# When the first expert's weights are loaded in an mLSTM-plus-MoE kernel: w1 in quarters in steps 19 and 21, w2 in step 22

## The chip, the cores and the metric

The kernel runs on one core of a Trainium2 chip. Times are device microseconds (us) of that core. The runs shown give the median of three executions; one more look comes from the hardware profiler, whose page and trace cover one execution.

## What is computed

The program has two halves. The first is an mLSTM cell over 4 batches, 8 heads, 768 time steps and heads of 40 elements. The second treats its output as 3072 token rows of 320 elements and sends each row to one of 8 experts by a hash of its token id; an expert is two matrix products with a ReLU between them. Cut to its core:

```python
for t in range(S):                       # S = 768, state C is 40 x 40 per head
    m_new = maximum(f_gate[t] + m, i_gate[t])
    f_stab, i_stab = exp(f_gate[t] + m - m_new), exp(i_gate[t] - m_new)
    C = f_stab * C + i_stab * outer(v[t], k[t])
    n = f_stab * n + i_stab * k[t]
    y[t] = sigmoid(o_gate[t]) * (C @ q[t]) / maximum(abs(n @ q[t]), 1)
x = y.reshape(3072, 320)                 # (batch, time) x (head, dim)
e = token_ids * 2654435761 % 8
out[rows of e] = relu(x[rows of e] @ w1[e]) @ w2[e]   # w1: 320x1024, w2: 1024x320
```

## The kernel before

**The cell** is cut into 24 steps (`NT`), one for each batch and each block of 128 time positions; step `s` works on batch `s % 4` and block `s // 4`. All engines run one hand-written order, a Python loop over `s`, with no scheduler between. In step `s` TensorE does, in this order: `turn(s + 2)`, which transposes the keys and queries of the block after next (L390); `scores(s + 1)`, the products of keys and queries (L447); `decays(s + 1)`, two products that build the logarithms of the decay weights (L405, tile `ab`) and, from the second block on, one for the queries' decay (L418, tile `xb`); `state(s)`, the update of C (L478); `attend(s)`, the output rows (L499 and L505). `decays` reads a tile called R, which holds rows of gate sums fetched from DRAM by `load_a` (L248). There are three R buffers, and `load_a(s + 3)` is issued in step `s`, so R(22) is fetched in step 19 and R(23) in step 20. VectorE makes `qs` (L422) from `xb`, and `weigh` (L453) multiplies scores by decay weights, which frees the two score tiles `sp0` and `sp1` for the next `scores`. ScalarE takes the exponentials (L414), copies the transposed blocks out (L395) and, in `gate(i)`, turns an output gate into a sigmoid (L438, L439). GpSimd multiplies the gate in (`gated`, L522). The finished rows go to a DRAM table `x_d` (`store`, L525), from SyncE's queue up to block 16 and from GpSimd's after that.

**The loads.** Nearly all DMAs are issued by SyncE (SP), in program order. Step `s` issues, in this order: `load_a(s + 3)`, k and q of block `s + 5`, v of block `s + 4`, the output gate (`og`) of a later block, one store, and then the `pieces` of the step. A load of k, q, v or og is 160 KB in 1024 runs of 160 bytes. The supply of blocks ends near the tail: step 18 has the last k and q, step 19 the last v, step 20 the last R. The program gives SP's DMAs eight completion semaphores in rotation, and each DMA waits for the one eight before it.

**The first expert's weights.** Expert 0 needs w1 (rows 0 to 255 as tile `w1t`, 1024 KB; rows 256 to 319 as `w1c`, two loads of 128 KB) and w2 (`w2t`, 1280 KB). `slices_of(0)` cuts these loads into seven `parts`, and the step loop hangs one into `pieces` of each of steps 17 to 23: w1's upper 128 rows in 17, its lower 128 rows in 18, `w1c` in 19, and a quarter of w2 in each of steps 20 to 23.

**The tail.** In step 20 GpSimd gathers two blocks of expert 0's rows from `x_d` (`xg0`, L110). They are copied by VectorE in step 22 (L886) and transposed by `early_turn` in steps 22 and 23 (L747, copied out at L748). When step 23 is over, `layer1(W[0], ...)` runs for the first 256 rows (L157 and L150): it takes the 1024 columns of w1 in four pairs of 128 (`fp`), from low to high. The expert loop follows: `layer2` for expert 0 (L1042), then for each further expert both layers with seven products in place of eight (L991, L999, L1075), fed by gathers on GpSimd, a pass through DRAM (`x_slots`, `xb`), and the weight loads of `load_weights` on SP.

Of the kernel before, what the change touches and what calls it, by code (L numbers as in the profile page):

```python
# [17 lines left out]
P = 128  # L18
# [4 lines left out]
def kernel(  # L23
# [24 lines left out]
    nc = tc.nc  # L48
# [5 lines left out]
    E, _, F = moe_w1.shape  # L54
# [65 lines left out]
    def slices_of(e):  # L120

        w1t = wpools[0].tile([P, 2, F], F32, name="w1t")
        w1c = wpools[0].tile([P, FB // 2, P], F32, name="w1c")
        w2t = w2pools[0].tile([P, FB, Dm], F32, name="w2t")
        W[e] = w1t, w1c, w2t
        last = moe_w1[e][2 * P :, :].rearrange("d (a two f) -> two d a f", two=2, f=P)
        rows = moe_w2[e].rearrange("(a p) d -> p a d", p=P)

        def part(i):
            if i < 2:  # L130
                nc.sync.dma_start(w1t[:, i], moe_w1[e][i * P : (i + 1) * P, :])
            elif i == 2:
                for j in range(2):
                    nc.sync.dma_start(w1c[j * P // 2 : (j + 1) * P // 2], last[j])
            else:
                r = slice(2 * (i - 3), 2 * (i - 2))
                nc.sync.dma_start(w2t[:, r], rows[:, r])

        return [lambda i=i: part(i) for i in range(7)]

    def layer1(w, xT, h, c0, c1, bank):

# [47 lines left out]
    with tc.tile_pool(name="gates", bufs=1) as gp, \  # L190
# [363 lines left out]
        def route_iotas(i):  # L554
            for ti, tf, pattern, base, mult in list(iotas.values())[i::2]:
                nc.gpsimd.iota(ti[:], pattern=pattern, base=base, channel_multiplier=mult)
                nc.gpsimd.tensor_copy(tf[:], ti[:])
# [140 lines left out]
        def route_table(i):  # L698
            tk = ps.tile([P, 2, NC], F32, name="tk", tag="sp0")
            for t in range(TH):  # L700
                nc.tensor.matmul(tk[:], lhsT=oh_r[:, t, :], rhs=oh_c[:, t], start=(t == 0), stop=(t == TH - 1))
            for part in range(2):
                if i == 0 and part == 0:
                    nc.vector.tensor_copy(tv[:], tk[:, 0])
                else:
                    nc.vector.tensor_tensor(tv[:], tv[:], tk[:, part], op=ALU.add)

        def route_index():
# [17 lines left out]
        pieces = {  # L726
            2: [lambda: route_iotas(0)], 3: [lambda: route_iotas(1), route_consts, route_parts], 4: [route_experts],
            5: [route_chosen], 7: [route_extra, route_masked], 8: [route_rank], 9: [route_high], 10: [route_slots, g2.ends, lambda: g2.split("e")], 11: [route_places],
            20: [route_index], 21: [route_tiles],
        }  # L730
        products = {4: [route_turned], 5: [route_counts]}
        for i in range(8):
            pieces.setdefault(12 + i, []).append(lambda i=i: route_hot(i))
            if i % 2:
                products[12 + i] = [lambda i=i // 2: route_table(i)]
        for i, part in enumerate(slices_of(0)):
            pieces.setdefault(17 + i, []).append(part)
        gates_of = {}
        for i, j in enumerate((4, 5, 6, 6, 7, 8, 8, 9)):
            gates_of.setdefault(j, []).append(i)  # L740
# [368 lines left out]
    with tc.manual_schedule():  # L1109
# [56 lines left out]
        for e in range(E):  # L1166
            g, i = e // EG, e % EG
# [84 lines left out]
```

## Time and profile before

| | |
|---|---|
| median of three runs | 357.02 us (353.64 to 359.27) |
| the profiled execution's own time | 357.02 us |
| its span | 355.2 us |
| TensorE busy | 336.3 us, 95% of the span |
| VectorE / ScalarE / GpSimd busy | 229.8 / 139.4 / 215.1 us |
| DMA traffic | 59.18 MB, mean 167 GB/s |
| mean granted TensorE clock | 0.988 |

Times in the trace count from the start of the span; the run's own time is 1.8 us longer. A busy share is an average over stages with different limits, so the stage around the change, from about 95 to 160 us, has to be read by itself.

### The profile page before, as it was taken

How to read it: one execution, taken by the hardware profiler on the slowest of the kernel's cores; microseconds unless marked ns; L12 is line 12 of the kernel's file. 1: busy time of each engine (PE TensorE's matmuls, PEld its weight loads, DVE VectorE, ACT ScalarE, POOL GpSimd, SP SyncE). 2: the span in 40 equal slices, each digit the busy share in tenths (PEclk: the TensorE clock that was granted, in tenths of full speed). 3: DMA queues.
4: the chain of work that ended last, by engine and by line, in shares of the span. 5: the costliest groups of instructions: out<-in, count | busy, mean ns of one | idle time of the engine just before them, and what ended most of it. 6: DMA issues, size and time to landing. Idle time of an engine off the chain costs nothing.

```text
span 355.2 us, 9214 instructions
## 1 busy us (share of the span) xinstructions
PE 336.3 (95%) x3573; PEld 293.8 (83%) x3573; DVE 229.8 (65%) x512; ACT 139.4 (39%) x325; POOL 215.1 (61%) x301
## 2 busy tenths in 40 slices
PE   7889999999999599999999999999999999999990
PEld 6677898888888476789899899789899899899870
DVE  8867897998888462037675796835776756844510
ACT  6676688776675451021411412301411412312300
POOL 8832778899885346515925938825926918427521
PEclk9999999999999899999999999999999999999997
DMA  6698999989988983679987959587477484000010
GB/s 129 118 195 156 162 200 172 194 175 193 177 165 199 243 239 92 198 201 297 218 247 192 327 103 316 159 215 219 117 208 237 106 235 146 0 34 22 16 40 3
DMA packets 162358, 59.18 MB, mean 167 GB/s; under 512 B 140171, under 2 KB 158119, under 8 KB 162313
## 3 DMA queue, kind: packets, MB, share of 16 engines
q1 hardware_dynamic: 158377, 49.05, 59.8%
q0 software_dynamic: 2832, 9.34, 8.0%
q8 instruction: 29, 0.48, 0.5%
q10 hardware_dynamic: 1104, 0.18, 0.3%
q14 instruction: 16, 0.13, 0.1%
HBM read 46.48 MB, written 12.38 MB: 166 GB/s over the span
## 4 chain that ended last, share of the span: by engine, by line
PE 84%; DMA 4%; issue 4%; DVE 3%; ACT 2%; SPq 1%; POOL 1%; POOLq 0%
PE mh L991 20%; PE mh L1075 13%; PE mh L1042 12%; PE sp L447 6%; PE mh L999 6%; PE tr L390 6%; PE xh L505 5%; PE mh L157 3%; PE ab L405 3%; PE xh L499 3%; PE xh L478 2%; DMA k<-in_k_dram 2%; DMA R<-gate_rows 1%; PE mh L1155 1%; PE xb L418 1%
## 5 line engine op out<-in xcount | busy, mean ns | idle before, releaser
L917 POOL DMA_INDIRECT out_dram<-zo,s_idx x26 | 26.8, 1030 | 69.5 <-issue 47.2
L1042 PE MATMUL mh<-w2t,h 128*128 128x320 f32 x160 | 45.0, 433 | 0.5 <-ACT h L166 0.5
L1042 PEld LDWEIGHTS mh<-w2t,h 128*128 128x128 f32 x160 | 30.0, 190 | 11.8 <-ACT h L166 0.9
L977 DVE TENSOR_TENSOR h<-u,mh 128x416 f32<-128x416 f32 (+1 forms) x56 | 25.4, 475 | 16.6 <-PE mh L999 7.8
L505 PE MATMUL xh<-v,w 128*64 128x41 f32 x768 | 35.6, 225 | 0.0
L414 ACT ACTIVATE w<-ab 128x512 f32<-128x512 f32 x48 | 26.2, 596 | 18.8 <-PE ab L405 17.9
L453 DVE TENSOR_TENSOR w<-sp,w 128x512 f32<-128x512 f32 x48 | 30.8, 681 | 3.6 <-ACT w L414 3.6
L991 PE MATMUL mh<-tx,sw 128*128 128x208 f32 x168 | 31.8, 339 | 0.0
L505 PEld LDWEIGHTS xh<-v,w 128*64 128x64 f32 x768 | 31.8, 141 | 0.0
L991 PEld LDWEIGHTS mh<-tx,sw 128*128 128x128 f32 x168 | 29.7, 190 | 0.0
L447 PE MATMUL sp<-qT,kT 64*128 64x128 f32 x384 | 28.0, 285 | 0.9 <-ACT qT L395 0.9
L110 POOL DMA_INDIRECT xg<-x_rows,g_idx x24 | 23.4, 974 | 9.0 <-issue 6.7
L977 DVE TENSOR_TENSOR u<-m,mh 128x416 f32<-128x416 f32 x28 | 16.5, 588 | 18.7 <-PE mh L991 18.0
L499 PE MATMUL xh<-C,qs 128*64 128x82 f32 x320 | 28.3, 254 | 0.0
L522 POOL TENSOR_TENSOR x<-x,og 128x320 f32<-128x320 f32 x24 | 20.6, 865 | 12.1 <-ACT og L439 10.1
L1075 PE MATMUL mh<-tw,sh 128*128 128x160 f32 x168 | 27.4, 299 | 0.0
L447 PEld LDWEIGHTS sp<-qT,kT 64*128 64x128 f32 x384 | 23.4, 187 | 4.8 <-issue 2.3
L1075 PEld LDWEIGHTS mh<-tw,sh 128*128 128x128 f32 x168 | 24.3, 190 | 0.0
L991 PE MATMUL mh<-xT,w1t 128*128 128x208 f32 x112 | 23.1, 339 | 0.0
L488 POOL TENSOR_TENSOR C<-C,add 64x164 f32<-64x164 f32 x32 | 16.3, 509 | 9.9 <-ACT add L482 8.6
L913 ACT COPY zo<-mh 128x320 f32<-128x320 f32 x12 | 5.1, 426 | 42.6 <-PE mh L1042 27.3
L422 DVE TENSOR_TENSOR qs<-qT,xb 128x512 f32<-128x512 f32 x20 | 13.7, 683 | 12.6 <-PE xb L418 12.6
(241 smaller groups left out, 775.3 us busy)
## 6 DMA issues: line engine op xcount, KB each, us to landing
w2t<-in_moe_w_dram SPq DMA_DIRECT2D x7, 1280.0 KB
w1t<-in_moe_w_dram SPq DMA_DIRECT2D x7, 1024.0 KB
xb<-x_slots SPq DMA_DIRECT2D x84, 52.0 KB
k<-in_k_dram SPq DMA_DIRECT2D x24, 160.0 KB
v<-in_v_dram SPq DMA_DIRECT2D x24, 160.0 KB
og<-in_o_gate_dram SPq DMA_DIRECT2D x24, 160.0 KB
q<-in_q_dram SPq DMA_DIRECT2D x23, 160.0 KB
x_slots<-xg SPq DMA_DIRECT2D x7, 480.0 KB
```

Of the source, the lines that this page charges most:

```text
L110: nc.gpsimd.indirect_dma_start(out=xg, out_offset=None, in_=x_d[:rows, :], in_offset=bass.IndirectOffsetOnAxis(ap=idx, axis=0),)
L390: nc.tensor.transpose(tp[:, j, :], d[what][:, 2 * j : 2 * j + 2, :].rearrange("p h d -> p (h d)"), ident[:])
L414: nc.scalar.activation(w[:, hf], ab[:], AF.Exp)
L447: nc.tensor.matmul(sp[hf][:, j, :], lhsT=d["kT"][r, j, :], rhs=d["qT"][r, j, :], start=True, stop=True)
L453: nc.vector.tensor_tensor(d["w"][:, hf], d["sp"][hf][:], d["w"][:, hf], op=ALU.mult)
L499: nc.tensor.matmul(xh[t, 2 * j : 2 * j + 2, :], lhsT=d["qs"][:, j, t], rhs=Cs[b][c % 2][:, j].rearrange("p h d -> p (h d)"), start=True, s ...
L505: nc.tensor.matmul(hs[t, 2 * j + hf, :], lhsT=d["w"][:, hf, j, t], rhs=d["v"][:, 2 * j + hf, :], start=(c == 0), stop=True, skip_group_che ...
L917: ins = nc.gpsimd.indirect_dma_start(out=out[:, :], out_offset=bass.IndirectOffsetOnAxis(ap=idx, axis=0), in_=zo[:], in_offset=None, bound ...
L977: nc.vector.tensor_tensor(o, a, b, op=ALU.add)
L991: nc.tensor.matmul(pair(bank[n])[:, a], lhsT=lhsT(g + a), rhs=rhs, start=first and a == 0, stop=True, skip_group_check=True,)
L1042: nc.tensor.matmul(zp, lhsT=h[:, fb, j * P : (j + 1) * P], rhs=w[2][:, fb, :], start=(fb == 0), stop=(fb == FB - 1),)
L1075: nc.tensor.matmul(bank[n], lhsT=lhsT(f), rhs=rhs(f), start=first and f == 0, stop=f == FB // 2 - 1, skip_group_check=True,)
```

## The change

The loads of w1's rows 0 to 255 are cut in four: each 128 rows by half of the columns (512 of 1024). The quarters with the low columns are issued in step 19, `w1c` in step 20, the quarters with the high columns in step 21, and all four parts of w2 in step 22. In every step they still stand behind the step's own loads. Nothing is issued in steps 17, 18 and 23 any more.

```diff
         def part(i):
-            if i < 2:
-                nc.sync.dma_start(w1t[:, i], moe_w1[e][i * P : (i + 1) * P, :])
-            elif i == 2:
+            if i < 4:
+                f = slice(i // 2 * F // 2, (i // 2 + 1) * F // 2)
+                nc.sync.dma_start(w1t[:, i % 2, f], moe_w1[e][i % 2 * P : (i % 2 + 1) * P, f])
+            elif i == 4:
                 for j in range(2):
                     nc.sync.dma_start(w1c[j * P // 2 : (j + 1) * P // 2], last[j])
             else:
-                r = slice(2 * (i - 3), 2 * (i - 2))
+                r = slice(2 * (i - 5), 2 * (i - 4))
                 nc.sync.dma_start(w2t[:, r], rows[:, r])
 
-        return [lambda i=i: part(i) for i in range(7)]
+        return [lambda i=i: part(i) for i in (0, 1, 4, 2, 3, 5, 6, 7, 8)]
...
-        for i, part in enumerate(slices_of(0)):
-            pieces.setdefault(17 + i, []).append(part)
+        for s, part in zip((19, 19, 20, 21, 21, 22, 22, 22, 22), slices_of(0)):
+            pieces.setdefault(s, []).append(part)
```

The instructions of the four computing engines and their order are the same in both programs; only SP's order differs:

| step | SP before | SP after |
|---|---|---|
| 17 | R(20), k, q, v, og, store, **w1 upper rows** | R(20), k, q, v, og, store |
| 18 | R(21), k(23), q(23), v(22), og(19), store(16), **w1 lower rows** | R(21), k(23), q(23), v(22), og(19), store(16) |
| 19 | R(22), v(23), og(20), **w1c x2** | R(22), v(23), og(20), **w1 low columns x2** |
| 20 | R(23), og(21), **w2** | R(23), og(21), **w1c x2** |
| 21 | og(22), og(23), **w2** | og(22), og(23), **w1 high columns x2** |
| 22 | **w2** | **w2 x4** |
| 23 | **w2** | nothing |

## The prediction

> **What bounds the kernel now.** I read the page's busy shares first, then TensorE's waits in the stretch of the change, then SP's issues there, then the granted clock.
>
> ```profile
> PE 336.3 (95%) x3573; PEld 293.8 (83%) x3573; DVE 229.8 (65%) x512; ACT 139.4 (39%) x325; POOL 215.1 (61%) x301
> ```
>
> TensorE is busy 95% of the span, so time can come only from its holes. The list of waits of PE between 100 and 140 us has one large one:
>
> ```profile
> PE ab L405 <- DMA R<-gate_rows: 3.6, 1, 3.6
> ```
>
> In the timeline of PE and of SP (start, length, what, idle before) that hole and its history read:
>
> ```profile
> 114.50 0.41 PE L505 MATMUL xh<-v,w 128*64 128x41 f32 x8
> 115.11 0.63 PE L390 MATMUL tr<-ident,k 128*128 128x128 f32 x4 [0.20 <-DMA k<-in_k_dram]
> 116.37 1.16 PE L447 MATMUL sp<-qT,kT 64*128 64x128 f32 x16
> 121.18 0.83 PE L405 MATMUL ab<-R,L 128*64 128x512 bf16 x4 [3.65 <-DMA R<-gate_rows]
> ...
> 126.13 0.62 PE L405 MATMUL ab<-R,L 128*64 128x512 bf16 x4
> ...
> 132.06 1.99 PE L157 MATMUL mh<-xT,w1t 128*128 128x256 f32 x8 [0.28 <-ACT xT L748]
> ```
>
> ```profile
> 107.26 0.42 SPq L131 DMA_DIRECT2D w1t<-in_moe_w_dram  x1
> 107.78 0.33 SPq L248 DMA_DIRECT2D R<-gate_rows  x1
> 108.15 0.59 SPq L237 DMA_DIRECT2D k<-in_k_dram  x1
> 108.79 0.88 SPq L237 DMA_DIRECT2D q<-in_q_dram  x1
> 109.72 4.55 SPq L237 DMA_DIRECT2D v<-in_v_dram  x1
> 114.36 0.53 SPq L233 DMA_DIRECT2D og<-in_o_gate_dram  x1
> 114.99 0.93 SPq L525 DMA_DIRECT2D x_rows<-x  x1
> 115.97 0.42 SPq L131 DMA_DIRECT2D w1t<-in_moe_w_dram  x1
> 116.48 0.31 SPq L248 DMA_DIRECT2D R<-gate_rows  x1
> ```
>
> The reader is to see that R(22), wanted at 117.5, is issued only at 116.48, behind both w1 loads, and that the issue of v(22) holds SP for 4.55 us just after the first w1 load. Last, the table of 2 us stretches (PE, PEld, DVE, ACT, POOL, clock, DMA share, GB/s):
>
> ```profile
> 118.00:120.00 2.00, 0.00 (x0) 0.00 (x0) 0.00 (x0) 1.54 (x4) 1.00 (x2) 1.00 0.89 236
> 122.00:124.00 2.00, 2.00 (x35) 1.86 (x32) 1.52 (x3) 1.48 (x5) 0.97 (x1) 0.50 0.96 227
> ```
>
> After the hole TensorE runs at half clock; the trace's clock record gives 0.5 from 121.46 to 124.87. After 162 us PE has no visible hole until the end, so what is gained by then arrives at the end if the expert's supply moves with it.
>
> [...]R(22) landed at 121.14, just after the w1 load issued before it (120.83). [...]the first w1 load landed on 15 engines by 112.15 and on the last at 114.47, and k(23) behind it by 112.97 and at 114.97. [...]3.65 us idle and then 3.41 us at half.
>
> **The change part by part.** The order of all computing engines is unchanged. I use the landing records of the semaphores.
>
> *Removed ahead of R(22): the first w1 load.* The DMA before it (store of block 15) had landed by 109.37, and on the late engine at 109.74; w1 landed by 112.15 and 114.47. It cost 2.4 to 2.8 us on most engines and 4.7 on the late one, part of that a 16 KB instruction fetch of 0.95 us and a GpSimd store, which stay. I take 2.3 to 2.8 us. With it the long issue of v(22) goes; in steps before, that issue took 0.6 to 1.0 us.
>
> *Removed ahead of R(22): the second w1 load.* Block 16's store landed by 118.06, this w1 by 120.12 and 120.83: 2.1 to 2.8 us.
>
> *Sum:* R(22) lands 4.4 to 5.6 us earlier, at 115.5 to 116.7.
>
> *When it is wanted.* k(23) and q(23) move up by 2.3 us or more and no longer hold PE. Step 21 starts at 114.91, transposes take 1.02 and scores 1.09 (the chain's durations), so `ab`(22) can start at 117.02. R(22) is there with 0.3 to 1.5 us to spare: the stall of 3.65 goes,[...] and the half clock goes too. At full clock L405, L418 and the attend products take 0.55 + 0.22 + 1.53 = 2.30 us; they took 3.93 (121.18 to 125.11), so that is 1.63. Waits for k and q give about 0.3.
>
> *What is late next.* `scores`(23) reuses the score tiles that `weigh`(22) frees. In the undisturbed step before, `ab` started at 107.45 and `weigh` ended at 110.21, 2.76 later. So the tiles are free at 119.8, not when attend ends at 119.3, and `ab`(23) starts at 119.8 + 1.09 = 120.9. It started at 126.13: a gain of 5.2 (3.65 + 1.63 + 0.3 less some 0.4 of this wait).
>
> *Added ahead of R(23): the two low-column quarters.* They have the bytes of one old w1 load; the trace shows no load in 2 KB runs, so I bound them by the two old ones, 2.1 to 2.8 us. Behind R(22), v(23) landed 0.5 and og(20) 1.3 us later. So R(23) lands 1.3 + 2.1 to 2.8 + 0.3 = 3.7 to 4.4 us after R(22), 119.2 to 121.1; middle 120.2, wanted at 120.9. I take no wait, and keep 0 to 1.5 us for the range. No other wait is new: each DMA's wait for the one eight before it finds that landed in this reckoning.
>
> *Moved: w1c, og(22), og(23).* From R(23) at about 120.2: og(21) 0.8, w1c 1.1 (122.41 to 123.53 before), the two gates 0.8 each, an instruction fetch 1.0: 124.7. ScalarE reaches gate(23) 4.55 us after `ab`(23) (130.68 less 126.13), at 125.4. Hidden, by 0.7; without that cover gate(23) holds the last copy (L748) before layer 1.
>
> *The gathers on POOL* wait for gate(19), whose load landed at 117.62 and now 2.3 or more earlier, 115.3. ScalarE takes 0.97, so `gated`(19) starts near 116.3 and not at 118.70. In the trace the second gather landed at 126.53, 7.83 after that start: 124.1 now. VectorE wants it 2.77 after `ab`(23), at 123.7. Cost 0 to 0.4.
>
> *Moved: high columns and w2.* 2.1 to 2.8, then four times 0.9 to 1.0 us (128.9 to 132.2 for three before): 127 and 131. Layer 1 starts 5.93 after `ab`(23), at 126.8, and reaches the high columns 4.9 later, 131.7; layer 2 starts near 137. Hidden with 4 to 6 us.
>
> *Behind layer 1.* w2 now shares the DMA engines with the last row stores, 2.1 us to landing before (134.31 to 136.41). I allow 0.3. From there the chain leads to expert 1's w1, landed at 160.42, wanted at 160.74: it absorbs 0.3 us.
>
> *Sum.* 5.2 less 0.2 for the gathers is 5.0. The profiled execution took 357.02 (span 355.2), so 352.0 (span 350.2). Its own time equals the median of the runs, so this is the prediction for both.
>
> **The rivals.**
>
> *R(23) takes the place of R(22).* For: the two quarters stand ahead of it as the second w1 load stood ahead of R(22), and one late engine was 1 to 2 us behind. Against: the queue is 4.4 us or more further ahead. At a wait of 2 us, or the same lost on gate(23) or the gathers: 354.2.
>
> *More than the stall goes.* TensorE's other visible holes from 100 to 142 us are about 1.5 us (0.5 before early_turn, 0.28 at layer 1, 0.47 at layer 2, k and q 0.3), and the slowest run shown, 359.27, may have stalled longer. With all of it and 0.5 of run-to-run luck: 350 or less, a gain of 7. Against: most of those holes are waits on VectorE and ScalarE, which the change does not touch.
>
> *Slower: the last R behind w1[...].* Should the quarters' 2 KB runs move at half the rate of the old 4 KB runs (no row shows it), they take 5 us, R(23) lands near 123, and the late engine adds 2 to 3:[...] w1's high columns, doubled too, hold layer 1. With a wait of 5: 352.0 + 5 + 1.6 = 358.6.[...]
>
> *The change does not do what it says.* If v(22)'s long issue came from the 160-byte loads and not from w1, R(22) gains only the 2.1 to 2.8 of the second w1 load and lands at 118.3 to 119.0: a stall of 1.3 to 2[...]. `ab`(23) gains about 3.5: 353.5.
>
> **How the numbers follow.** The forecast has 0.55 at 352.0; R(23) or a gate next 0.14 at 354.2; the half effect 0.08 at 353.5; more than the stall 0.16 at 350 or less; slower 0.07. Runs of before spread by 2 to 3 us about their median, which widens each case alike. The range 349.0 to 356.5 holds the forecast with this spread, both smaller gains and part of the larger, and leaves out about 0.15. A gain over 2% means 349.9 or less, 7.1 us, about what a measurement of this kernel can tell from no change; a slowdown over 2% means 364.2. So faster by over 2%: 0.25, the larger gain and the lower tail of the forecast; slower 0.05, the long end of the slower rival; within 2% 0.70.
>
> **What would show it.** In the profile after: no w1 load before SP's L248 of step 19; v(22) issued in about 1 us; no wait of `ab` for R(22) over 0.5; the clock at 1.0 from 100 to 160; `ab`(23) near 121 and L157 near 127; the span shorter by about 5. It is wrong if PE waits over 1 us for R(23), for the gathers or for a gate, if L157 waits for w1 or L1042 for w2, or if the half clock stays.

## The result and the profile after

On the chip of the first comparison the changed kernel took 353.88 us (median of 20 runs, 352.84 to 356.3) and the kernel before 356.35 us (20 runs, 353.36 to 359.27): ratio 0.9948, 95% interval 0.9925 to 0.9971. The profiled execution of the changed kernel took 353.61 us, its span 351.8. So the kernel became faster by 0.5% by this ratio and by 2.5 us in the medians, where the prediction had 5.0. Two later comparisons, told below, gave 0.9979 (0.9955 to 1.0003) and 0.9958 (0.9939 to 0.9977), with 0.9 and 1.4 us between the medians. The medians are those of all runs, while the ratios leave out runs more than 1.5% above the fastest of their kernel.

Line numbers behind the diff are one higher than before: L405 is now L406, L157 is L158, L991 is L992. The page's busy shares of the changed kernel:

```profile
PE 335.3 (95%) x3573; PEld 292.8 (83%) x3573; DVE 229.8 (65%) x512; ACT 138.6 (39%) x325; POOL 214.6 (61%) x301
```

TensorE lost 1.0 us of busy time and the span 3.4. SP's issues in the stretch of the change (start, length, what):

```profile
107.65 0.29 SPq L249 DMA_DIRECT2D R<-gate_rows  x1
108.00 0.39 SPq L238 DMA_DIRECT2D k<-in_k_dram  x1
108.44 0.66 SPq L238 DMA_DIRECT2D q<-in_q_dram  x1
109.15 2.44 SPq L238 DMA_DIRECT2D v<-in_v_dram  x1
...
113.06 0.30 SPq L249 DMA_DIRECT2D R<-gate_rows  x1
...
114.57 1.82 SPq L132 DMA_DIRECT2D w1t<-in_moe_w_dram  x2
116.50 0.29 SPq L249 DMA_DIRECT2D R<-gate_rows  x1
```

R(22) (the last R but one in these lines) is issued at 113.06, with no w1 load ahead of it; before it was 116.48. v(22) still takes 2.44 us to issue, not the 1 us that was foretold. PE's timeline of the same execution, cut to the lines that answer those shown of before:

```profile
117.11 0.62 PE L406 MATMUL ab<-R,L 128*64 128x512 bf16 x4
121.14 0.77 PE L406 MATMUL ab<-R,L 128*64 128x512 bf16 x4
...
124.52 0.33 PE L748 MATMUL tpx<-ident,xg 128*128 128x128 f32 x1 [0.54 <-DVE xg L887]
125.26 0.52 PE L748 MATMUL tpx<-ident,xg 128*128 128x128 f32 x3 [0.41 <-DMA xg<-x_rows,g_idx]
127.51 1.99 PE L158 MATMUL mh<-xT,w1t 128*128 128x256 f32 x8
...
159.42 2.38 PE L992 MATMUL mh<-tx,sw 128*128 128x208 f32 x12 [0.87 <-DVE sw L948]
```

The wait for R(22) is gone, and `ab`(22) and `ab`(23) start at 117.11 and 121.14 (foretold 117.02 and 120.9). Layer 1 starts at 127.51, where it was 132.06: 4.55 us gained. But the last line is a wait that the profile of before did not have: 0.87 us, for `sw`, sums and differences of blocks of expert 1's w1 that VectorE makes for the layers with seven products. With it, and what else is lost on the way, 3.4 of the 4.55 us reach the end. The table of 2 us stretches (PE, PEld, DVE, ACT, POOL, clock, DMA share, GB/s) for the two stretches shown of before:

```profile
118.00:120.00 2.00, 1.89 (x50) 1.60 (x44) 1.94 (x4) 1.65 (x5) 1.23 (x2) 1.00 0.77 227
122.00:124.00 2.00, 1.98 (x51) 1.69 (x47) 1.97 (x5) 1.60 (x5) 0.62 (x1) 1.00 1.34 217
```

TensorE has no hole at 118 and the clock is 1.00 (full) at 122. So the pair of profiles shows what was foretold in the stage of the change, and less at the end; and the medians differ by less than the profiles. The experiments ask why.

### The profile page after: what moved, and what is told of

The parts are those of the page before. It is cut to its first block, busy times and chain, and to the rows that moved or that the text cites. A ratio compares the mean times of both kernels' runs of the same rounds, so it can differ in the third digit from the quotient of the medians.

```text
span 351.8 us, 9217 instructions
## 1 busy us (share of the span) xinstructions
PE 335.3 (95%) x3573; PEld 292.8 (83%) x3573; DVE 229.8 (65%) x512; ACT 138.6 (39%) x325; POOL 214.6 (61%) x301
## 4 chain that ended last, share of the span: by engine, by line
PE 76%; DMA 7%; issue 6%; DVE 4%; SPq 2%; ACT 2%; POOL 1%; ACTq 0%; POOLq 0%
PE mh L992 20%; PE mh L1076 14%; PE mh L1043 9%; PE sp L448 7%; PE mh L1000 6%; PE tr L391 6%; PE xh L506 4%; PE ab L406 3%; PE xh L500 3%; DMA w1t<-in_moe_w_dram 3%; PE xh L479 2%; SPq L1138 2%; DMA xg<-x_rows,g_idx 2%; PE mh L1156 1%; DMA x_rows<-x 1%
## 5 line engine op out<-in xcount | busy, mean ns | idle before, releaser
L506 PE MATMUL xh<-v,w 128*64 128x41 f32 x768 | 34.8, 222 | 0.0
L992 PE MATMUL mh<-tx,sw 128*128 128x208 f32 x168 | 31.9, 340 | 0.9 <-DVE sw L948 0.9
L506 PEld LDWEIGHTS xh<-v,w 128*64 128x64 f32 x768 | 30.9, 138 | 0.0
L992 PEld LDWEIGHTS mh<-tx,sw 128*128 128x128 f32 x168 | 29.7, 190 | 1.2 <-DVE sw L948 1.2
L500 PE MATMUL xh<-C,qs 128*64 128x82 f32 x320 | 27.5, 249 | 0.0
L992 PE MATMUL mh<-xT,w1t 128*128 128x208 f32 x112 | 23.1, 339 | 0.0
L1006 ACT COPY m<-mh 128x416 f32<-128x416 f32 x14 | 7.1, 505 | 38.3 <-PE mh L992 24.9
```

The costliest lines, as they stand in the source:

```text
L500: nc.tensor.matmul(xh[t, 2 * j : 2 * j + 2, :], lhsT=d["qs"][:, j, t], rhs=Cs[b][c % 2][:, j].rearrange("p h d -> p (h d)"), start=True, s ...
L506: nc.tensor.matmul(hs[t, 2 * j + hf, :], lhsT=d["w"][:, hf, j, t], rhs=d["v"][:, 2 * j + hf, :], start=(c == 0), stop=True, skip_group_che ...
L992: nc.tensor.matmul(pair(bank[n])[:, a], lhsT=lhsT(g + a), rhs=rhs, start=first and a == 0, stop=True, skip_group_check=True,)
```

## The experiments

The theory after the result: the stall on R(22) is not in every execution. The profiled execution of before had it in full, so it overstated what there was to gain. Its rivals: the stall is in every execution and the gain is lost again at expert 1; or the gain has to do with w2, or with where the bytes of w1 lie, and not with R.

### The kernel before once more

No edit. 

> The kernel before, unchanged, for a second profile of it and the granted clock of each of its runs. Theory U (the profiled execution of before was not typical[...]): this profile shows a shorter wait of ab for R, 1 to 3 us, no half clock in the middle, and half of the runs or more have a clock of 0.991 or above. Theory G (the gain up to layer 1 is typical, and most of it is given back later in the expert chain): the wait is again[...] with a half clock after it, and nearly all runs have a clock of 0.989 or less.

It took 354.41 us (22 runs), ratio 0.9991 (0.9969 to 1.0013). The PE timeline of this execution:

```profile
117.76 0.62 PE L405 MATMUL ab<-R,L 128*64 128x512 bf16 x4
121.73 0.62 PE L405 MATMUL ab<-R,L 128*64 128x512 bf16 x4
127.66 1.99 PE L157 MATMUL mh<-xT,w1t 128*128 128x256 f32 x8 [0.23 <-ACT xT L748]
...
159.40 2.38 PE L991 MATMUL mh<-tx,sw 128*128 128x208 f32 x12 [0.71 <-DVE sw L947]
```

The unchanged kernel has no wait for R(22) here, reaches layer 1 at 127.66 and `sw` at 159.40, and its span is 351.8: at these lines it is within 0.7 us of the profile of the changed kernel. Even the new wait for `sw` is there, and in the three profiles of the next section it comes again, with 1.0, 0.5 and 0.6 us. So that wait does not come from the change.

### Three more profiles of the kernel before

No edit in any of them. 

> The kernel before, unchanged, one more profiled execution. Theory of an intermittent stall: one such look in three shows PE waiting over 3 us for R(22) with a half clock after it, and a span of about 355; the others show no wait for R over 1 us and a span of about 352. Rival (the stall is in every execution and the second profile was the exception): all of the looks show it.

> The kernel before, unchanged, another profiled execution; the same two expectations as for the look before it: one in three with the stall and a span of about 355, or all of them.

> The kernel before, unchanged, another profiled execution; the same two expectations: one in three with the stall and a span of about 355, or all of them.

These are the third, fourth and fifth profile of the kernel before. The issue of v(22) in SP's timeline and PE's `ab`(22), from the third, the fourth and the fifth (which has no wait for R):

```profile
108.28 2.90 SPq L237 DMA_DIRECT2D v<-in_v_dram  x1
...
118.92 0.62 PE L405 MATMUL ab<-R,L 128*64 128x512 bf16 x4 [1.88 <-DMA R<-gate_rows]
```

```profile
110.22 4.32 SPq L237 DMA_DIRECT2D v<-in_v_dram  x1
...
122.02 1.07 PE L405 MATMUL ab<-R,L 128*64 128x512 bf16 x4 [4.21 <-DMA R<-gate_rows]
```

```profile
108.61 1.68 SPq L237 DMA_DIRECT2D v<-in_v_dram  x1
...
118.56 0.62 PE L405 MATMUL ab<-R,L 128*64 128x512 bf16 x4
```

All five profiles of before, in the order of the stall (the first is that of the prediction). The last column but one is the time from `ab`(21), ahead of the stall in each, to the first product of layer 1, so that shifts from earlier in the run drop out:

| profile of before | v(22)'s issue | wait for R(22) | half clock after it | `ab`(21) to L157 | span |
|---|---|---|---|---|---|
| second | 1.50 us | none | none | 14.37 | 351.8 |
| fifth | 1.68 | none | none | 15.18 | 353.3 |
| third | 2.90 | 1.88 | none | 16.40 | 353.3 |
| first | 4.55 | 3.65 | 3.41 us | 19.47 | 355.2 |
| fourth | 4.32 | 4.21 | 6.83 us | 21.40 | 358.0 |

The expectation of "one in three in full, the others none" was too simple: the stall was 0, 0, 1.88, 3.65 and 4.21 us, and only the two longest were followed by the half clock. It is long where the issue of v(22), which holds SP just behind the first w1 load, is long, though the two longest are not in the same order. The profile of the prediction is the second worst of five. The middle span is 353.3, 1.9 below the one that the prediction started from.

### w1 alone, and w2 alone

The first has w1 as in the changed kernel and w2's parts in steps 20 to 23 as before (its diff is against the changed kernel); the second has w1's loads as before and all of w2 in step 22 (against before, as in the three experiments that follow it).

```diff
-        for s, part in zip((19, 19, 20, 21, 21, 22, 22, 22, 22), slices_of(0)):
+        for s, part in zip((19, 19, 20, 21, 21, 20, 21, 22, 23), slices_of(0)):
...
-        for i, part in enumerate(slices_of(0)):
-            pieces.setdefault(17 + i, []).append(part)
+        for s, part in zip((17, 18, 19, 22, 22, 22, 22), slices_of(0)):
+            pieces.setdefault(s, []).append(part)
```

> w1 in quarters in steps 19 and 21 and w1c in step 20 as after the change, but w2 in steps 20 to 23 as before. Theory G with w2's burst as the cause: the row stores of blocks 21 to 23 land in 2.1 to 2.5 us again and not in up to 4.3, the wait for sw in the first seven-product layer (0.87 us) goes, ratio to before about 0.991. If instead w1's move as such pushes all later bytes back, so that w2 ends at the same 131.6 us wherever its quarters stand: same as the change, 0.995, with the wait for sw still there. Theory U says nothing on w2: 0.995.

> w1 in steps 17 and 18 and w1c in step 19 as before; only w2 goes to step 22. Nothing ahead of R(22) changes, so both theories keep its stall: ratio 1.000, within 0.003. If w2's quarter in step 20 was what delayed the gates of blocks 22 and 23, slightly faster, 0.998; if the burst hurts the row stores by itself, slower, 1.003.

w1 alone: 354.37 us (14 runs), ratio 0.9979 (0.9956 to 1.0003). w2 alone: 354.52 us, 1.0003 (0.9975 to 1.0031). Neither profile has a wait for R. In the second this is luck, as in two of the five profiles of before, since its w1 loads stand where they stood before. The two cannot be told apart well, as each interval holds 1, but the point estimates put what there is on w1's side. w2 could hardly matter: in the first profile of before the last three of its four parts, of steps 21 to 23, are already issued back to back from 124.30 on.

The profile of w1 alone shows something else. Its PE timeline:

```profile
125.24 0.84 PE L748 MATMUL tpx<-ident,xg 128*128 128x128 f32 x3 [0.85 <-DMA xg<-x_rows,g_idx]
126.50 0.52 PE L748 MATMUL tpx<-ident,xg 128*128 128x128 f32 x3 [0.42 <-DMA xg<-x_rows,g_idx]
...
129.18 2.99 PE L158 MATMUL mh<-xT,w1t 128*128 128x256 f32 x8
```

The transposes of expert 0's rows wait for GpSimd's gathers, 1.27 us together, and layer 1's first eight products take 2.99 us in place of 1.99: the trace's clock record has a half-clock stretch from 127.83 to 131.24.

### Only the upper rows of w1 moved

The upper 128 rows of w1 go from step 17 to step 19, whole; the lower rows stay in step 18, ahead of R(22).

```diff
-        for i, part in enumerate(slices_of(0)):
-            pieces.setdefault(17 + i, []).append(part)
+        for s, part in zip((19, 18, 19, 20, 21, 22, 23), slices_of(0)):
+            pieces.setdefault(s, []).append(part)
```

> Only the first w1 load (upper rows) goes, from step 17 to step 19; the second stays in step 18 ahead of R(22), w1c in 19, w2 in 20 to 23. By the prediction's sum R(22) gains 2.3 to 2.8 us of the 4.4 to 5.6. Under U (typical stall about 2 us) that is all of it: ratio 0.995 to 0.996 like the change. Under G (typical stall 3.65[...]) 0.9 to 1.3 us of stall is left: layer 1 starts 0.9 to 1.3 us later than after the change, and the ratio is about 0.997.

354.78 us (22 runs), ratio 0.9992 (0.9969 to 1.0016): no difference, so neither of the two ratios expected came, because a wait came in that neither had reckoned with. R(22) is in time and R(23), which now has a w1 load and `w1c` ahead of it, is not:

```profile
123.86 0.62 PE L405 MATMUL ab<-R,L 128*64 128x512 bf16 x4 [2.64 <-DMA R<-gate_rows]
```

This is the prediction's first rival, R(23) in the place of R(22), in one profile. Here it comes about when half of w1 is moved from in front of one R to in front of the next.

### All of w1 in step 17

The suspect doubled: both halves of w1's rows and both `w1c` loads in step 17, w2 as before.

```diff
-        for i, part in enumerate(slices_of(0)):
-            pieces.setdefault(17 + i, []).append(part)
+        for s, part in zip((17, 17, 17, 20, 21, 22, 23), slices_of(0)):
+            pieces.setdefault(s, []).append(part)
```

> The suspect doubled: both w1 loads and both w1c loads in step 17, ahead of R(21) and R(22); w2 as before. S with the w1 loads as the cause: R(21), wanted near 113, lands 3 to 4 us later than in before, PE waits 1 to 4 us for R(21) in most runs, the share of runs with a clock below 0.991 passes 50%, and the median rises by 2 to 4 us (ratio 1.006 to 1.011). If the late DMA engine or the instruction fetches make the stall without w1's help: like before, ratio 1.000.

356.34 us (22 runs), against 354.89 of before beside it; ratio 1.0022 (0.9995 to 1.005), so less than the 1.006 to 1.011 expected, and an interval that holds 1. The place of the stall is as expected: now R(21) is late, by 2.08 us:

```profile
PE ab L405 <- DMA R<-gate_rows: 2.1, 1, 2.1
```

11 of the 22 runs had a mean granted clock below 0.991. Of the 20 profiles of this document the six below that value (0.983 to 0.990) are the six with a half-clock stretch before the last 10 us (the first profiles of before and after fall to half clock there too, at 350.15 and 347.34 us), so the clock of a run hints at whether it had one. Of the kernel before it was 66 of 217 runs (30%) in all comparisons where the clock was recorded, and of the changed kernel 8 of 63 (13%). But the count does not tell what the half clock came from: of the six stretches two follow a wait for R, two a wait for gathers (w1 alone, and one told below), one lies at 13 us (fifth profile of before, mean clock 0.988) and one at expert 1. Nor is it steady: of the changed kernel it was 1 of 20, 7 of 22 and 0 of 21 runs, where before had 21 of 59 beside the 7 and 16 of 42 beside the 0. And the kernels told here that also have no w1 ahead of R(22) stay near the share of before: w1 alone 6 of 14, w1 by rows 7 of 22, the later bulk 6 of 22. So this count by itself does not show that less w1 ahead of an R leaves fewer runs at a lower clock.

### w1 by rows, behind R(22) and R(23)

As the changed kernel, but cut by rows alone: upper rows in step 19, `w1c` in 20, lower rows in 21, w2 in 22.

```diff
-        for i, part in enumerate(slices_of(0)):
-            pieces.setdefault(17 + i, []).append(part)
+        for s, part in zip((19, 21, 20, 22, 22, 22, 22), slices_of(0)):
+            pieces.setdefault(s, []).append(part)
```

> As the change, but w1 whole in 4 KB runs: upper rows in step 19, lower rows in step 21. It halves what stands ahead of R(23) and lets layer 1 wait for all of the lower rows, which should land near 126, wanted at 127.5. If the quarters do not matter: like the change, 0.995 to 0.998, no wait of L157. If the lower rows come late: L157 waits 0.5 to 2 us and the time rises by as much.

354.14 us (22 runs), ratio 0.9984 (0.996 to 1.0008), against 353.97 and 0.9979 for the changed kernel in the same comparison. The cut by columns is worth nothing that these runs can measure. The profile of this kernel waits 1.92 us at L747 for the second gather and has no half clock.

### The changed kernel again, and the floor at expert 1

> The changed kernel again, beside the kernel before on the same chip, for the granted clock of every run of both. The theory that now stands (S): the stall on R(22) comes in a part of the runs only; the change takes it from those and gives the others nothing. So of before about 30% of the runs have a clock below 0.991 and of this one 5 to 10%; among the runs of clock 0.991 or more the two differ by less than 0.5 us; the upper quartile falls by 1 us or more; ratio 0.995 to 0.998. The rival (T: every run gains, and the profile after shows a typical 3.4 us, part of it hidden by chance): the runs of high clock also differ by 1.5 us or more.

353.97 us (22 runs), ratio 0.9979 (0.9955 to 1.0003). The ratio and the fall of the upper quartile (356.2 to 355.0 us) came as expected. The share of runs at the lower clock did not: 7 of 22, and not 5 to 10%. And among the runs at a clock of 0.991 or more the medians differ by 0.6 us (354.4 and 353.9), in the last comparison below by 0.9 (355.1 and 354.2), so the change gives something to runs without a half clock too. The list of PE's waits from 100 to 165 us is led by the wait for `sw`:

```profile
PE mh L992 <- DVE sw L948: 1.0, 1, 1.0
```

The chain of waits of the first profile after (start, length, what), cut to the pieces that matter, leads to this wait:

```profile
127.68 4.29 DMA x_rows<-x
...
134.08 3.02 DMA xr<-x_rows,g_idx
...
142.80 2.73 DMA x_slots<-xg
145.52 0.30 SPq L1138
...
151.51 0.47 SPq L1138
151.98 0.04 issue
152.03 5.30 DMA w1t<-in_moe_w_dram
157.32 0.02 issue
157.35 0.69 DVE sw L946
158.04 0.61 DVE sw L947
158.65 0.02 issue
158.68 0.70 DVE sw L948
```

Expert 1's w1 is issued behind the twelve `xb` loads, and these wait for expert 1's rows: the last row stores, the gathers, the pass through DRAM. The next experiment took the weights off this chain: expert 1's w1 and `w1c` are issued ahead of its rows' passage and its w2 behind the `xb` loads.

```diff
-        eng.dma_start(w2t[:], src2.rearrange("(a p) d -> p a d", p=P))
+        if not split:
+            eng.dma_start(w2t[:], src2.rearrange("(a p) d -> p a d", p=P))
...
+        W[1] = weights(moe_w1[1], moe_w2[1], wpools[1], w2pools[1], split=True)
...
-        load_weights(1)
+        nc.sync.dma_start(W[1][2][:], moe_w2[1].rearrange("(a p) d -> p a d", p=P))
```

> The changed kernel, with expert 1's w1 and w1c issued on SP before fetch(1) in place of after its twelve xb loads; its w2 stays behind them. If the wait of TensorE for sw (0.71 to 0.87 us in three profiles without a stall) is the floor that the change runs into, w1 of expert 1 lands by about 148, VectorE starts sw at 156.6 in place of 157.35, the wait falls to about 0.1, and the time is 0.7 to 0.9 us below the change. If the gathers on GpSimd suffer from the megabyte beside them, the xb loads land later by as much and nothing is won or 1 us lost.

360.96 us (6 runs), ratio 1.0172 (1.0131 to 1.0213): 6 us worse than before, and worse than the bad branch of what was expected. PE's waits and SP's timeline:

```profile
PE mh L993 <- DVE xT L1143: 3.3, 1, 3.3
PE mh L993 <- DVE sw L949: 2.3, 1, 2.3
```

```profile
143.93 0.38 SPq L1124 DMA_DIRECT2D x_slots<-xg  x1
151.99 6.02 SPq L1139 DMA_DIRECT2D xb<-x_slots  x12
```

With the megabyte ahead of it the `x_slots` store, issued at 143.93, lets the `xb` loads go only at 151.99; in the changed kernel they start at 145.52. The two waits are followed by a half-clock stretch from 162.81 to 169.63, so part of the 6 us is the clock. The rows' passage did not bear this load ahead of it, and the wait for `sw` stays.

### The R loads alone moved

The other way to part R from w1: w1 and w2 stay where they are, and the 24 KB loads of R(21), R(22) and R(23) are issued at the ends of steps 17, 18 and 19, ahead of that step's w1 or `w1c`.

```diff
-            if s + 3 < NT and s not in (1, 2):
+            if s + 3 < NT and s not in (1, 2, 18, 19, 20):
                 load_a(s + 3)
...
                 decays(s + 1)
+            if s in (17, 18, 19):
+                load_a(s + 4)
+            for piece in behind.get(s, []):   # w1 and w1c
+                piece()
```

> The kernel before with only the small R loads moved: R(21), R(22) and R(23) are issued at the end of steps 17, 18 and 19, each ahead of that step's w1 or w1c load; w1 and w2 themselves stay in their steps. Theory of an intermittent stall (a late R behind w1 in a third of the runs): R(22) loses the lower w1 ahead of it, 2.1 to 2.8 us, so where it was late by 3.65 it is late by about 1[...]; runs with a granted clock below 0.991 fall from a third to a quarter or less, and their median comes down by 1 to 2 us; the runs without stay as before, so the median is 0.3 to 1.0 us below before, ratio 0.997 to 0.999. Rival (k, q and v behind the upper w1 are what is late, R only the last of them): a third or more of the runs stay at the lower clock, at 2 us above the others, and the ratio is 1.000. Rival (the change's gain comes from w1 and w2 no longer lying beside other traffic): also 1.000.

354.98 us (22 runs), ratio 1.0012 (0.9987 to 1.0036): no gain, and 12 of 22 runs below a clock of 0.991, with a median 2.6 us above that of the others (357.1 and 354.5), much as the first of the two rivals had it. Its profile has no wait for R. Two more profiles were to say what is late in the runs at the lower clock.

> The kernel with R(21), R(22) and R(23) issued one place earlier, unchanged, one more profiled execution, to see where its runs at the lower clock lose time. If k and q of block 23, issued behind the upper w1, are what is late there: PE waits 2 us or more at L390 for k or q, and the half clock follows. If R is late all the same: PE waits 2 us or more for R(21) or R(22). If the lower clock comes from elsewhere in the program: no wait over 1 us between 100 and 130 us, and a half clock before 100 us.

> The kernel with R(21), R(22) and R(23) issued one place earlier, another profiled execution; the same three expectations: a wait of 2 us or more for k or q, the same for R, or a half clock elsewhere.

Neither fell on such a run: spans of 351.5 and 350.9, no wait for R, no half clock, 1.3 us for a gather in the first of them. The second is the shortest span of all profiles here. What lowers the clock in half of this kernel's runs is not known. In this order R(22) still has the upper rows of w1 ahead of it and R(23) the lower rows, so R can be late here too; or something else behind w1 is late, as k, q and v. No profile here shows either.

### Two more profiles of the changed kernel

> The changed kernel, unchanged, one more profiled execution. Theory (the change takes the w1 loads away from in front of R(22), so no execution of it has the long stall): no wait of PE for R over 1 us, no half clock between 100 and 160 us, a wait of 0.7 to 1.1 us for sw of expert 1, a span of 351.4 to 352.5. Rival (late loads come from something else, and the changed kernel has them as often): a wait for R(22) or R(23) of 2 us or more in one of these looks.

> The changed kernel, unchanged, another profiled execution; the same two expectations: no wait for R over 1 us and a span of 351.4 to 352.5, or a wait for R of 2 us or more.

These are the third and fourth profile of the changed kernel. Neither has a wait for R. But the third has a span of 356.0 and a half clock, which was not expected. Its PE timeline, and the table by stretches around the wait:

```profile
125.54 0.63 PE L748 MATMUL tpx<-ident,xg 128*128 128x128 f32 x3 [1.08 <-DMA xg<-x_rows,g_idx]
127.89 0.88 PE L748 MATMUL tpx<-ident,xg 128*128 128x128 f32 x3 [1.72 <-DMA xg<-x_rows,g_idx]
...
131.66 2.81 PE L158 MATMUL mh<-xT,w1t 128*128 128x256 f32 x8
```

```profile
124.00:126.00 2.00, 0.92 (x19) 0.69 (x15) 1.27 (x3) 0.75 (x2) 0.85 (x1) 1.00 1.03 383
126.00:128.00 2.00, 0.28 (x2) 0.14 (x2) 0.22 (x2) 1.73 (x5) 0.60 (x1) 0.63 0.80 287
128.00:130.00 2.00, 2.00 (x25) 1.67 (x27) 0.90 (x4) 0.89 (x2) 0.84 (x1) 0.50 0.04 15
```

The transposes wait 2.80 us for the two gathers, and the half clock is back, for 6.83 us. While they wait the DMA engines move 383 and 287 GB/s: w1's high columns and w2, which SP has issued early here,

```profile
116.49 2.56 SPq L132 DMA_DIRECT2D w1t<-in_moe_w_dram  x2
119.09 2.06 SPq L138 DMA_DIRECT2D w2t<-in_moe_w_dram  x4
```

before and beside the first gather, which GpSimd issues at 119.3. So the changed kernel has a varying stall of its own. Its five profiles (the fifth is from the last experiment), in the order of this stall:

| profile after | w1's high columns issued | L748's waits for the gathers' DMA | half clock after it | `ab`(21) to L158 | span |
|---|---|---|---|---|---|
| second | 120.31 | none | none | 14.36 | 351.4 |
| fifth | 118.92 | none | none | 14.98 | 351.6 |
| first | 120.59 | 0.41 us | none | 14.87 | 351.8 |
| fourth | 116.14 | 1.69 | none | 15.64 | 352.1 |
| third | 116.49 | 2.80 | 6.83 us | 17.95 | 356.0 |

The two with the bulk (w1's high columns and w2) issued from 116 on are the two with the long waits. Two profiles of other kernels do not fit this order. With w1 alone moved the high columns were issued only at 121.49 (with a quarter of w2 at 119.47), and the gathers were waited for all the same, 1.27 us. In the second of the two more profiles with R alone moved, the last three parts of w2 were issued from 118.14 on, beside the first gather at 118.16, and there was no such wait:

```profile
121.49 3.69 SPq L132 DMA_DIRECT2D w1t<-in_moe_w_dram  x2
```

```profile
118.14 2.82 SPq L137 DMA_DIRECT2D w2t<-in_moe_w_dram  x3
```

From `ab`(21) to layer 1 the mean of the five is 15.56 us, against 17.36 for before: 1.8 us, and the best of both is the same, 14.36 and 14.37. The mean spans, 352.6 and 354.3, differ by 1.7.

### The bulk behind the gathers

As the changed kernel, but ScalarE issues w1's high columns at the end of its step 21 and w2, in two halves, at the end of its step 22.

```diff
-                nc.sync.dma_start(w1t[:, i % 2, f], ...)
+                (nc.sync if i < 2 else nc.scalar).dma_start(w1t[:, i % 2, f], ...)
...
-                r = slice(2 * (i - 5), 2 * (i - 4))
-                nc.sync.dma_start(w2t[:, r], rows[:, r])
+                r = slice(4 * (i - 5), 4 * (i - 4))
+                nc.scalar.dma_start(w2t[:, r], rows[:, r])
...
+            for piece in behind.get(s, []):   # behind gate(s - 1) of steps 21, 22
+                piece()
```

> The changed kernel with the bulk behind the low columns moved later: the two high-column quarters of w1 are issued by ScalarE at the end of its step 21 (near 121 us), w2 in two halves by ScalarE at the end of its step 22 (near 125 us), where SP issued them at 116.5 to 121 in the profiles with a late gather. Theory (in the changed kernel this bulk lies beside GpSimd's gathers of expert 0's rows and makes them late by 0 to 2.8 us, the more the earlier SP gets to it): no wait of L748 for xg over 0.5, L158 14.4 to 14.8 us after ab(21), w1 high landed by 126 and w2 by 132; fewer runs at the lower clock and a median 0.7 to 1.5 us below the changed kernel run beside it. Rival (the gathers are late for another reason, their own packets or the row stores): L748 waits for xg as before, and the median is that of the changed kernel. Rival (ScalarE's four issues of some 0.5 us each hold its exponentials or the last copies): a wait on ScalarE of 0.5 to 2 us in steps 22 and 23, or w2 late at L1043, and a median 0.5 to 2 us above.

> The changed kernel, unchanged, beside the kernel before and the one with the later bulk on the same chip. Theory: ratio to before between 0.994 and 0.999, as in the two comparisons already made. Rival (the gain of the first comparison came from the chip): 1.000 with an interval that reaches above 1.001.

The later bulk took 354.77 us (22 runs), the changed kernel 354.18 (21 runs), before 355.6: ratios to before 0.9974 (0.9952 to 0.9997) and 0.9958 (0.9939 to 0.9977). The gain expected of the later bulk did not come, and its runs below a clock of 0.991 were 6 of 22, where the changed kernel beside it had none of 21. In the profile of the later bulk the DMA of the second gather is still late; VectorE's and PE's timelines:

```profile
126.74 0.19 DVE L890 COPY xg<-xg 128x64 f32<-128x64 f32 x1 [1.28 <-DMA xg<-x_rows,g_idx]
```

```profile
126.86 0.52 PE L749 MATMUL tpx<-ident,xg 128*128 128x128 f32 x3 [1.01 <-ACT og L439]
```

(PE's wait is put down to ScalarE, but VectorE's copy of the gathered rows ended only at 126.9; it is the gather that PE waited for.) ScalarE issued the high columns at 119.94, just before the second gather's 120.24, so they still lay beside it. In layer 1 PE then waits another 1.15 us for VectorE (L165), which is held by a copy that waits 4.83 us for a later gather (L935); no profile of the changed kernel has that wait. That the bulk is what makes the gathers late therefore rests on the order of the five profiles, which the two lines above do not follow, and is not shown. The medians of the two kernels lie 0.6 us apart in favour of the changed one, but their intervals overlap. What is shown is that the gain of the changed kernel over before holds in a third comparison.

## Why the prediction was right or wrong

*The stall on R(22) and the half clock that follows: right in mechanism.* In the first profile after R(22) is issued 3.4 us earlier, and `ab`(22) starts within 0.1 us of the foretold time. None of the five profiles after waits for R, nor do the three of the other kernels that leave no w1 ahead of R(22) (w1 alone, w1 by rows, the later bulk), where three of the five of before do; and in the two kernels where more of w1 was put ahead of another R, that one was late (one profile each). So R was late behind w1 in three kernels here: before (1.88 to 4.21 us), the upper rows alone moved (2.64) and all of w1 in step 17 (2.08).

*R(23), the gates, the high columns, w2: right.* In none of the five profiles after does PE wait for any of them.

*"Its own time equals the median of the runs, so this is the prediction for both": the step that failed.* The 357.02 us were the median of three runs, and the time of one execution that had the stall in full. The time being that of the median run did not make the stall that of the median run. Of five profiles of before the stall of 3.65 us and its half clock are the second worst, and 30% of the timed runs had a clock below 0.991. The same steps applied to the middle profile (a wait of 1.88, no half clock, span 353.3) would have foretold, by an estimate from its wait alone, a gain near 2 us, and the measured ones are 2.5, 0.9 and 1.4 in the medians. The term that was mis-sized is "3.65 + 1.63 + 0.3": over the five profiles of before the time from `ab`(21) to L157 exceeds the undisturbed 14.37 by 3.0 us in the mean, not by 5.1. The cost of the gathers, told next, takes 1.2 of it back, and the 1.8 left are the mean gain at layer 1.

*"Cost 0 to 0.4" for the gathers: too small.* L748 waited 0, 0, 0.41, 1.69 and 2.80 us for their DMA in the five profiles, 1.0 in the mean, and once the half clock came with it; a wait over 1 us for the gathers was one of the signs of being wrong that the prediction named. Layer 1 came 1.2 us later in the mean than the best 14.36. The step reckoned when the gathers would be issued and let them take as long as in the profile of before; it did not ask what is now issued beside them. In the worst case they took 6.1 and 7.1 us to land, against 3.4 and 4.2 in the first profile of before. There the late R had also held up what reads the gathered rows, by 3.65 us and the half clock, which could hide a later landing.

*"It absorbs 0.3 us" for expert 1's w1: right in kind, too generous, and not what made the gain small.* The first profile after waits 0.87 us for `sw`; of the five, four wait 0.6 to 1.0, and the third, which reaches layer 1 last, does not. The step missed that the supply chain of expert 1 did not come forward as far as layer 1 did: w1 of expert 1 landed 3.1 us earlier, and layer 1 started 4.55 us earlier. But four of the five profiles of before have this wait too, 0.5 to 1.0 us, and only the one of the prediction has none. In the means the two kernels lose alike there, so it is part of the gap between that one profile and the medians.

*The rivals.* R(23) in the place of R(22) did not happen in the changed kernel, but it did, with 2.64 us, when one half of w1 stayed ahead of R(22). That the long issue of v(22) would stay was right in one profile of five: 2.44 us in the first after, with no w1 load ahead of it, and 0.71 to 1.38 in the others, where the five of before have 1.50 to 4.55. The half clock that the slower rival reckoned with came, for 6.83 us in one profile of five, behind another DMA than the rival named.

What is settled: the two kernels take the same time to layer 1 when nothing is late; R is late behind w1 in the kernel before, in some executions and by varying amounts; and the change takes that stall away and has a smaller one in its place, at the gathers. Open is why the lateness varies, what lowers the clock in half the runs of the kernel with only R moved, and what makes the gathers late in some executions. Five profiles of each kernel are few, so the means above are rough.

## What to carry to other kernels

A stall in one profiled execution is a sample: before its length is put into a forecast, look at the same wait in several executions, or at the spread of the runs, and use the middle one. When a large load is moved from in front of one small urgent transfer, list every other small transfer that it then lies beside, those of other queues too; here a stall came back among them, 1.2 us in the mean for 3.0. And a gain in one stage is kept only as far as the next stage's supply chain moves with it: of the 4.55 us between the first two profiles 3.4 were left at the end.

## What the hardware showed that was not expected

- A half-clock stretch came behind waits much shorter than the 3.65 us ahead of it in the first profile of before. With w1 alone moved, gaps of 0.85 and 0.42 us around a few transposes were followed by half clock from 127.83 to 131.24; in the third profile after, gaps of 1.08 and 1.72 us by half clock from 126.52 to 133.35. In the fourth profile after gaps of 0.59, 0.37 and 1.10 us had none. The ends of products are modelled in the trace, so the gaps may be longer than they look.
- In the first profile of before the stretches between the changes of the clock record are 116.05, 3.41 and 225.28 us long, which is 34, 1 and 66 steps of 3.41 us; in the first after the one at full clock is 341.33, 100 such steps; and the half-clock stretches told above lasted 3.41 or 6.83 us, one step or two. In the step of 3.41 us just ahead of the half clock TensorE was busy 0.28 of the 3.41 us in the first profile of before, and 2.06 with w1 alone moved, 1.98 in the third profile after and 2.51 ahead of the stretch at 13 us in the fifth of before. Busy time alone does not decide it: steps with 1.58 us busy (third profile of before, around the wait of 1.88) and 1.70 (upper rows alone, around the wait of 2.64) were not followed by half clock. What does decide is not shown.
- The same program's issue of the same 160 KB load took from 1.50 to 4.55 us in five executions, and the wait behind it from 0 to 4.21 us.
- In the first profile after one row store took 4.29 us to land, while w1 and w2 were being loaded (2.1 to 3.2 for the last four in the first profile of before); the gathers took up to 7.1 us, in the third profile after (3.4 to 4.2 in the first of before). That the loads beside them are the reason is not shown.
